# Gated mix of attention and a squared-ReLU layer: phases of six or four scores in place of six or eight, products split over two phases, and VectorE's side work placed by a clock kept while the program is written

## The chip, the cores and the metric

One NeuronCore of a Trainium2 chip runs the whole kernel. The metric is the device time of one execution in microseconds; the times below are those of separate runs of the same program. TensorE (PE), VectorE (DVE), ScalarE (ACT), GpSimd (POOL) and the queue of SyncE (SP) each work through their own list of instructions in the order in which the program wrote them, and wait for one another by semaphores.

## The reference

For 2048 tokens of width 512, one input x goes through two branches, mixed by a gate for each token:

```
g = sigmoid((x * gate_w).sum(-1))
q = x @ wq          # 32 heads of 16
k, v = x @ wk, x @ wv        # one head of 16, shared by all
a = softmax(q k^T * 16**-0.5) v, heads joined, @ wo
h = relu(x @ w1 + b1) ** 2   # 1792 wide
b = h @ w2 + b2
out = g * a + (1 - g) * b
```

All of it is float32; the kernel reaches that accuracy in products by splitting each operand into a rounded part (`r`) and a rest (`l`) and adding three products of them.

## The kernel before, in words

**Attention.** The work is cut into 32 groups (`it`): four heads with 512 tokens of queries each. A group has 32 units `u`: one block of 128 keys against one half (256 columns) of the queries, for all four heads. A unit's score is two matmuls on the two row halves of the array (`r` = 0, 1; `score`, L720), whose results go to a pair of PSUM banks `s` (two buffers; L727) and from there through exp on ScalarE to `e` in SBUF (L751). Some units go another way: each half goes to the single PSUM bank `x`, VectorE copies it to `e` (L738), and exp then runs in place. `context` (L754) multiplies the exps of a block of units with the values and adds in the bank `acc`; it runs four units behind the scores (`AHEAD`).

**Products.** Everything else that TensorE does comes in units of up to twelve products (`pairs`, three for each 128 rows of a term): 15 units for the queries, 56 units `hidden` (L614), `summed` (L635) with twelve or nine products, and the output projection (`outproj`, L199). Each unit's products run on row half 0 in one phase, and again, with the other 64 rows, on half 1 in the next, while the following unit takes half 0. So in each place of a phase two matmuls run side by side: a *pair* of scores, or of products.

**Phases.** `phase` (L1028) writes one phase: at its head a side step or two, then the pairs of scores and products by a text from `PLANS` for (scores, products), in which `S0` is a score, `M` a product, `02`/`12` the two halves of unit 2 for `x`, and `t` a place for VectorE's side work (`tick`, L595); last the exps in a given order. At the end `done` of the unit that has run on both halves reads its bank `mm` on VectorE. Then the caller writes the context of the block. `block` (L1096) says how many units that is: eight in stretches with room, otherwise six, four near the end of a group, and two at the kernel's end. A phase of eight sends its units 4 and 5 through `x`. Where no plan fits, `plain` puts a score every fourth place.

**Side work.** VectorE also splits weights (`w_rest`, L461; ScalarE rounds them first, L468), splits inputs loaded again (`x_again`, L656) and attention results (`ask`), and divides finished groups by their sums in six parts of four instructions (`divide`, L769-L776, called by `pieces`). `tick` takes one job at each `t`; the divisions go one part for each call of `steps_aside` at a phase's head. A job that follows a load waits until a rough clock, which counts phases, has moved on by 6 us.

**Queues.** SyncE issues the loads of weights (L451), of the queries (`q_load`, L424: eight loads at each group's start), and the moves of a finished group's sums (`unpack`, L195, which waits for ScalarE's copy `accs`). Also the load of `ress` into `ot` for the projection (`ahead`, L205; in the trace `big<-ress`), issued at the head of the phase in which the unit's second half runs; its reader is L208.

Of the kernel before, what the change touches and what calls it, by code (L numbers as in the profile page):

```python
# [35 lines left out]
LANDS = 6.0  # L36
GROUPS = (0, 1, 2, 3), (4, 5, 6, 7), (8, 9, 10), (11, 12, 13)
AHEAD = 4
PLANS = {
# [115 lines left out]
def mix_kernel(ctx: ExitStack, tc: tile.TileContext, xT, wkv, wq, wo, w12, b1, b2, cst, out):  # L155
# [42 lines left out]
    def outproj(c, ots, orr, orl, wor, wol):  # L198
        for j in range(4):  # L199
            cols = slice(j * 128, (j + 1) * 128)  # L200
            s = 4 * c + j
            ot = ots[j % 2]

            def ahead(j=j, ot=ot):
                nc.sync.dma_start(ot, ress[c][:, j])  # L205

            def done(p, s=s, ot=ot):
                nc.vector.scalar_tensor_tensor(ot, p, g[:, s:s + 1], ot, op0=OP.mult, op1=OP.add)  # L208
# [10 lines left out]
    with fast, tc.tile_pool(name="at", bufs=1) as at, \  # L219
# [159 lines left out]
        def q_unit(c, t):  # L379

            def done(p):
# [3 lines left out]
                sq = sq8[:, c % 2 * KT + t]  # L385
                nc.vector.tensor_tensor(sq, qr.bitcast(F32), qr.bitcast(F32), OP.mult)
# [51 lines left out]
        clock = 0.0  # L438

        def w_load(half):  # L440
            n = len(wf[half])
            if n < NC * NF:
# [7 lines left out]
                since[half][n] = clock  # L450
# [4 lines left out]
        def w_round(half, copy):  # L455
# [3 lines left out]
            copy(rounded[half][n][0], wf[half][n])  # L459

        def w_rest(half):  # L461
            n = len(ws[half])
            r, l = ws[half][n] = rounded[half][n]
            nc.vector.tensor_tensor(l, wf[half][n], r.bitcast(F32), OP.subtract)
            wanted.append(half)
# [12 lines left out]
        def w_ready(half):  # L478
            n = len(rounded[half])
            return (n == len(ws[half]) and n in since[half] and n < min(room[half], NC * NF)  # L480
                    and clock - since[half][n] > LANDS)
# [77 lines left out]
        for t in (2, 3):  # L559
# [13 lines left out]
        chores, soon = [], [lambda: wq_rest(3), lambda: k_shift(2), lambda: (k_shift(3), w_load(0), w_load(1)),  # L573
                         lambda: (wq_round(0), wq_rest(0))]
        soon += [lambda: (w_load(0), w_load(1))] + [lambda k=k: x_split(2, k) for k in range(KT)]
        soon += [lambda k=k: x_split(3, k) for k in range(KT)] + [gate]
        ring, h, b2t, x, osp = [], [], [], dict(enumerate(zip(xr, xl))), {}

        def later(f, *args):
            chores.append(lambda: f(*args))  # L580
# [5 lines left out]
        def steps_aside(n):  # L586

            for _ in range(n):
                if side and next(side[0], "end") == "end":
                    side.pop(0)  # L590

        def rests():
            return [half for half in halves() if len(rounded[half]) > len(ws[half])]

        def tick(early):  # L595

            nonlocal held
            if soon:
                if early:
                    soon.pop(0)()  # L600
                    if soon and len(es) > 16:
                        soon.pop(0)()
                return
            if not early:
                for half in rests()[:1]:
                    return w_rest(half)
            if chores and clock > held:
                if chores.pop(0)():
                    held = clock + 6.0
# [4 lines left out]
        def hidden(c, f, hs):  # L614
# [3 lines left out]
            while c not in x:  # L618
                chores.pop(0)()
# [3 lines left out]
            def done(p):  # L623
# [3 lines left out]
                split(hr, hl, h[0])  # L627
                room[0] += 1
# [27 lines left out]
        def x_again(c):  # L656
# [11 lines left out]
            for k in range(KT):  # L668
                if k % 2 == 0:
                    chores.append(lambda k=k: load(k // 2))  # L670
# [34 lines left out]

        parts, copied, fifth = {}, {}, [None] * 4
# [20 lines left out]
        def score_part(u, r):  # L727

            if u not in parts:
                parts[u] = [sp.tile([128, 2, CH], F32, name="s"), 0]  # L730
            score(u, r, parts[u][0][:, r])
            parts[u][1] += 1

        def score_copy(u, r):

            x = aside()
            score(u, r, x)
            nc.vector.tensor_copy(e_half(u)[:, 2 * r:2 * r + 2], x.rearrange("p (a n) -> p a n", a=2))  # L738
            copied[u] = copied.get(u, 0) + 1

        def exps(todo):

            while todo:
                u = todo[0]
                if copied.get(u) == 2:
                    src = e_half(u)
                elif u in parts and parts[u][1] == 2:
                    src = parts[u][0].rearrange("p r (a n) -> p (r a) n", a=2)
                else:
# [4 lines left out]
        def context(acc, us):  # L754

            while us:
                u, (it, kt, q) = us[0], place(us[0])
                n = 2 if u % 2 == 0 and len(us) > 1 and it < NC * NG - 1 else 1
                us = us[n:]
                cols, mine = slice(q * HC, (q + n) * HC), slice(u % 2 * HC, (u % 2 + n) * HC)  # L760
                for h in range(4):
                    nc.tensor.matmul(acc[h * 32:(h + 1) * 32, cols], v_ext[:, kt],  # L762
                                     es[u // 2][:, h % 2 * 2 + h // 2, mine], start=(kt == 0), stop=(kt == NK - 1),
                                     skip_group_check=True, tile_position=(0, h * 32))

# [3 lines left out]
        def divide(t, o, l, cols, okc):  # L769

            n = at.tile([128, 86], F32, name="n")[:, :cols.stop - cols.start]
            nc.vector.tensor_scalar(n, l[:, cols], L_MIN, L_MAX, op0=OP.max, op1=OP.min)
            nc.vector.scalar_tensor_tensor(l[:, cols], n, 1.0, l[:, cols], op0=OP.mult, op1=OP.is_equal,  # L773
                                           accum_out=okc)
            nc.vector.reciprocal(n, n)  # L775
            nc.vector.tensor_tensor(o[:, cols], o[:, cols], n, OP.mult)  # L776

        def finish(it, acc):
# [9 lines left out]
            nc.scalar.activation(a, acc, AF.Copy)  # L788
            if u == 0:
                ol[c, t] = [at.tile([128, CH], F32, name=n) for n in ("oc", "lc")]  # L790
            o, l = ol[c, t]
            unpack(nc.sync, o[u * 64:u * 64 + 64], l[u * 64:u * 64 + 64], a)
            if u == 1:
                side.append(pieces(it, c, t, o, l))

        def pieces(it, c, t, o, l):
            for _ in range(2):
                yield
            for q, cols in enumerate(PARTS):
                i = len(PARTS) * (4 * c + t) + q  # L800
                divide(t, o, l, cols, ok[:, i:i + 1])
                if q < len(PARTS) - 1:
                    yield
            nc.gpsimd.dma_start(oTs[it - 1:it + 1].rearrange("u d n -> (u d) n"), o)
            complete.add((c, t))
# [3 lines left out]
        def turn(a, u, js, okc, idle=0):  # L809
# [8 lines left out]
            for j in range(m):  # L818
                nc.tensor.transpose(tp[:, j], a[:, j * 128:(j + 1) * 128], ident)
                if m > 2 and j % 2:  # L820
                    yield
# [55 lines left out]
        def o_ready(c):  # L877

            if c == 0 and not wos:
# [6 lines left out]
                for t in range(KT):  # L886
                    if t % 2 == 0:
                        chores.append(lambda t=t: load(t // 2))
                    chores.append(lambda t=t: split(wos[0][:, t], wos[1][:, t], stage()[:, t % 2]))
# [3 lines left out]
        def ask(c, n=KT):  # L893
# [21 lines left out]
            for t in range(n):  # L915
                if t % 2 == 0:
                    chores.append(lambda t=t: load(t // 2))
                later(part, t)

        def ask_one(c, t):  # L920
# [14 lines left out]
            chores.extend((load, part))  # L935
# [83 lines left out]
        phases, scored, before, evicted = 0, 0, None, None  # L1019
# [8 lines left out]
        def phase(unit, n):  # L1028

            nonlocal phases, scored, before, evicted, clock  # L1030
            halves_of = (unit[0] if unit else ()), (before[0] if before else ())
            slots = max(map(len, halves_of))
            if unit and len(unit[0]) > 6:
                units_left[0] -= 1
            clock += 0.36 + 0.429 * n + 0.2345 * (n + slots)
            full = slots > 8
            tick(True)
            steps_aside(2 if full else 1)
            if narrow:
                qnorm(narrow.pop(0))  # L1040
            if before and before[1][1]:
                before[1][1]()
            if before and not (unit and evicted):
                nc.vector.tensor_copy(at.tile([128, 1], F32, name="peek"), before[2][:, :1])  # L1044
            here = mp.tile([128, CH], F32, name="mm") if unit else None
            text, order = PLANS.get((n, slots)) or plain(n, slots)
            rows, ticks, done = ([], []), {}, [0, 0]
            for item in text.split():
                if item == "t":
                    ticks[len(rows[0])] = True  # L1050
                elif item[0] == "0":
# [8 lines left out]
            def product(r):  # L1060

                i = done[r] - (slots - len(halves_of[1]) if r else 0)
                done[r] += 1
                if 0 <= i < len(halves_of[r]):
                    a, b = halves_of[r][i]
                    p = slice(64 * r, 64 * r + 64)
                    nc.tensor.matmul(before[2] if r else here, a[p], b[p], start=not r and i == 0,  # L1067
                                     stop=r == 1 and i == len(halves_of[r]) - 1, skip_group_check=True)

            for i in range(len(rows[0])):  # L1070
                for r in range(2):
                    item = rows[r][i]
                    if item == "M":
                        product(r)
# [5 lines left out]
                if i in ticks:  # L1080
                    tick(False)
# [3 lines left out]
            phases += 1  # L1085
            evicted = before
            if before:
                before[1][0](before[2])
            before = (unit[0], unit[1:], here) if unit else None
# [6 lines left out]
        def block(u, unit):  # L1096

            k = u % (2 * NK)
            rest = 2 * NK - k
            if u >= total - 2 * NK:  # L1100
                rest = NK - u % NK
# [89 lines left out]
```

## Time and profile before

| | us |
|---|---|
| median of 3 runs | 1315.5 |
| lowest, highest | 1312.73, 1318.16 |
| the profiled execution's own time | 1312.76 |
| its span in the trace | 1311.0 |
| busy: PE, ACT, DVE | 1255.7, 1065.5, 760.4 |

The span runs from the first to the last instruction of the trace; the execution's time is 1.8 us longer. PE's busy time counts every moment in which at least one matmul is recorded as running. In the chain of waits a line gives the start, the length, the engine, the tile that is written and the line of the kernel; in grouped waits a row gives the waiting instruction, what it waited for, the sum in us, the number of times and the longest.

### The profile page before, as it was taken

What the parts mean: (1) busy time and instruction counts of PE and PEld (TensorE: products, weight loads), DVE (VectorE), ACT (ScalarE), POOL (GpSimd) and SP (SyncE); (2) the same over time, 40 slices, a digit from 0 to 9 for tenths busy, and PEclk for the clock granted to TensorE, in tenths of its full rate; (3) what the DMA queues carried; (4) which work ended last, traced back from release to release, by engine and by line L of the source; (5) the groups of instructions that cost most, each with busy time, mean ns of one, the idle gap of its engine ahead of it and who ended that gap; (6) DMA issues with size and microseconds to landing.
All of it is one profiled execution on the core that took longest, in us unless ns stands there. A gap on an engine that the chain in (4) does not pass through costs nothing.

```text
span 1311.0 us, 24220 instructions
## 1 busy us (share of the span) xinstructions
PE 1255.7 (96%) x9839; PEld 673.7 (51%) x9839; DVE 760.4 (58%) x1461; ACT 1065.5 (81%) x1193; POOL 58.7 (4%) x75
## 2 busy tenths in 40 slices
PE   9899899999999999999989998999999999999997
PEld 4555455455545555554545555554555555555454
DVE  5564775657384843738456663655738376464632
ACT  5676788888878888788978887888888888878875
POOL 1010110000001000000002000000000100000000
PEclk9999999999999999999999999999999999999999
DMA  6233521211132213102122222111112121211010
GB/s 207 85 99 80 154 70 30 67 48 52 35 109 78 77 53 102 41 22 78 45 86 82 68 77 78 45 53 46 57 63 69 53 86 38 86 47 37 22 50 35
DMA packets 46117, 88.72 MB, mean 68 GB/s; under 512 B 10642, under 2 KB 10898, under 8 KB 45488
## 3 DMA queue, kind: packets, MB, share of 16 engines
q1 hardware_dynamic: 38752, 71.42, 17.6%
q0 software_dynamic: 7104, 15.44, 3.4%
q8 instruction: 79, 1.29, 0.4%
q14 instruction: 38, 0.31, 0.1%
q10 hardware_dynamic: 144, 0.26, 0.1%
HBM read 57.83 MB, written 20.97 MB: 60 GB/s over the span
## 4 chain that ended last, share of the span: by engine, by line
PE 68%; DVE 12%; ACT 12%; issue 3%; DMA 3%; SPq 1%; ACTq 0%; DVEq 0%
PE acc L762 24%; PE mm L1067 23%; PE s L724 14%; ACT e L751 10%; PE x L724 5%; DVE n L775 2%; DVE e L738 2%; SPq L424 1%; DVE lc L773 1%; DVE big L625 1%; DVE big L626 1%; DMA lc<-accs 1%; DMA big<-ress 1%; ACT w2r L468 1%; DVE hr L184 1%
## 5 line engine op out<-in xcount | busy, mean ns | idle before, releaser
L751 ACT ACTIVATE e<-s 128x1024 f32<-128x1024 f32 x826 | 804.4, 1027 | 217.7 <-PE s L724 126.6
L738 DVE COPY e<-x 128x512 f32<-128x512 f32 x396 | 273.5, 691 | 392.4 <-PE x L724 302.8
L762 PE MATMUL acc<-e,v_ext 128*32 128x512 f32 (+1 forms) x4224 | 475.1, 585 | 0.0
L724 PE MATMUL s<-qa,k_aug 49*128 49x512 f32 x1652 | 431.6, 437 | 14.2 <-ACT e L751 13.4
L724 PEld LDWEIGHTS s<-qa,k_aug 49*128 49x128 f32 x1652 | 208.6, 186 | 224.2 <-ACT e L751 187.8
L762 PEld LDWEIGHTS acc<-e,v_ext 128*32 128x32 f32 x4224 | 121.1, 110 | 259.0 <-issue 255.3
L1067 PE MATMUL mm<-w2r,hr 64*128 64x512 f32 x896 | 219.6, 395 | 0.1
L751 ACT ACTIVATE e<-e 128x1024 f32<-128x1024 f32 x198 | 209.9, 1060 | 0.0
L724 PE MATMUL x<-qa,k_aug 49*128 49x512 f32 x396 | 164.5, 415 | 22.2 <-DVE e L738 19.3
L1067 PEld LDWEIGHTS mm<-w2r,hr 64*128 64x128 f32 x896 | 130.5, 187 | 14.6 <-DVE peek L1044 0.6
L1067 PE MATMUL mm<-w2l,hr 64*128 64x512 f32 x448 | 135.4, 395 | 0.0
L724 PEld LDWEIGHTS x<-qa,k_aug 49*128 49x128 f32 x396 | 74.4, 188 | 54.0 <-DVE e L738 41.3
L1067 PE MATMUL mm<-xragain,w1r 64*128 64x512 f32 x224 | 70.5, 399 | 5.5 <-DVE big L208 5.5
L1067 PEld LDWEIGHTS mm<-w2l,hr 64*128 64x128 f32 x448 | 71.9, 186 | 6.3
L1067 PE MATMUL mm<-xragain,w1l 64*128 64x512 f32 x224 | 74.3, 399 | 0.0
L1067 PE MATMUL mm<-xr,w1l 64*128 64x512 f32 x224 | 72.8, 398 | 0.0
L1067 PE MATMUL mm<-xlagain,w1r 64*128 64x512 f32 x224 | 70.5, 397 | 0.0
L1067 PE MATMUL mm<-xr,w1r 64*128 64x512 f32 x224 | 67.8, 396 | 1.9 <-DVE big L208 1.9
L1067 PE MATMUL mm<-xl,w1r 64*128 64x512 f32 x224 | 68.4, 395 | 0.0
L775 DVE RECIPROCAL n<-n 128x86 f32<-128x86 f32 x90 | 61.9, 688 | 3.1
L648 DVE SCALAR_TENSOR_TENSOR res<-mm,omg,res 128x512 f32<-128x512 f32 x64 | 47.8, 746 | 14.1 <-PE mm L1067 13.9
L625 DVE TENSOR_SCALAR big<-mm,b1t 128x512 f32<-128x512 f32 x56 | 41.8, 746 | 9.8 <-PE mm L1067 9.8
(156 smaller groups left out, 1123.1 us busy)
## 6 DMA issues: line engine op xcount, KB each, us to landing
stage<-in_w SPq DMA_DIRECT2D x56, 256.0 KB
qa<-qs SPq DMA_DIRECT2D x186, 64.0 KB
w1f<-in_w SPq DMA_DIRECT2D x28, 256.0 KB
w2f<-in_w SPq DMA_DIRECT2D x28, 256.0 KB
qs<-qr SPq DMA_DIRECT2D x16, 256.0 KB
ress<-res POOLq DMA_DIRECT2D x4, 1024.0 KB, 4.3
qs<-ql POOLq DMA_DIRECT2D x15, 256.0 KB, 8.2
oc<-accs SPq DMA_DIRECT2D x30, 128.0 KB
```

What stands on the lines that cost most here:

```text
L184: nc.vector.tensor_tensor(l, src, r.bitcast(F32), OP.subtract)
L424: nc.sync.dma_start(q[64 * r + row:64 * r + row + b - a].bitcast(F32), qs[it, r, a:b])
L468: nc.scalar.activation(out, src, AF.Copy)
L625: nc.vector.tensor_scalar(h[0], p, b1t[:, f:f + 1], 0.0, op0=OP.add, op1=OP.max)
L626: nc.vector.tensor_tensor(h[0], h[0], h[0], OP.mult)
L648: nc.vector.scalar_tensor_tensor(part, p, omg[:, s:s + 1], part, op0=OP.mult, op1=OP.add)
L724: nc.tensor.matmul(dst.rearrange("p (a n) -> p a n", a=2), k_aug[rows, kt * 128:(kt + 1) * 128], qa[it][rows, :, q * HC:q * HC + HC], star ...
L738: nc.vector.tensor_copy(e_half(u)[:, 2 * r:2 * r + 2], x.rearrange("p (a n) -> p a n", a=2))
L751: nc.scalar.activation(e_half(u), src, AF.Exp, scale=SCALE)
L762: nc.tensor.matmul(acc[h * 32:(h + 1) * 32, cols], v_ext[:, kt], es[u // 2][:, h % 2 * 2 + h // 2, mine], start=(kt == 0), stop=(kt == NK ...
L775: nc.vector.reciprocal(n, n)
L1067: nc.tensor.matmul(before[2] if r else here, a[p], b[p], start=not r and i == 0, stop=r == 1 and i == len(halves_of[r]) - 1, skip_group_ch ...
```

## The change

Phases have six scores or four; none has eight. A unit's products are no longer bound to one phase: a `Span` holds the unit on half 0 and the one before it on half 1, and `phase(slots, n, m)` takes all its product places (`WHOLE`, with six scores) or half of them (`FIRST` and `SECOND`, with four scores each). `block` decides by how many units of attention and of products are left: a counter `halved` grows with the surplus, and at 1 a span is halved. Every plan sends one unit of four or six through `x`, and its exp comes last or second to last. The first phase writes six scores and takes the next one four.

While the program is written, three numbers (`at_pe`, `at_act`, `at_dve`) count the time of each engine by fixed prices. The `t` places are gone; before each copy of `x`, before a unit's bank is read, and after a phase without such a copy, `spend(until)` writes side work whose end fits before that moment. A division is four jobs in place of one part. Rounding of weights can go to VectorE when ScalarE has no room. `ahead` is issued from GpSimd, at the start of the span in which its unit takes half 0. The phases of the whole program: before, 47 phases of eight scores with twelve products, 8 of eight with nine, 71 of six with twelve, 17 of six with nine; now 80 of six with twelve, 23 of six with nine, 85 of four with six, and some smaller ones.

```diff
 PLANS = {
-    (8, 12): ("S0 M 04 S1 M M M M M S2 M t 14 S3 M M M M 05 M t M S6 M S7 15", (0, 1, 2, 3, 4, 6, 7, 5)),
-    (6, 12): ("S0 M M S1 02 M t M M M M S3 M t 12 M M S4 M M S5", (0, 1, 3, 4, 2, 5)),
+    (6, 12, WHOLE): ("M 02 S0 M S1 M M M M M S3 M M M S4 12 M M S5", (0, 1, 3, 4, 5, 2)),
+    (4, 6, FIRST): ("M 02 S0 M M S1 M M M 12 S3", (0, 1, 3, 2)),
...
             def ahead(j=j, ot=ot):
-                nc.sync.dma_start(ot, ress[c][:, j])
+                nc.gpsimd.dma_start(ot, ress[c][:, j])
...
+        def spend(until=None):
+            nonlocal held
+            def fits(d, ready=0.0):
+                return until is None or max(at_dve, ready) + d <= until
+            while True:
+                due = [i for i in halves() if len(rounded[i]) > len(ws[i])]
+                if due and fits(0.68, since[due[0]][len(ws[due[0]])]):
+                    w_rest(due[0])
+                elif soon and fits(soon[0][1]):
...
+                elif divisions and fits(*divisions[0][:2]):
+                    d, ready, f = divisions.pop(0)
+                    dve(d, ready)
+                    f()
+                elif chores and fits(chores[0][0], held):
+                    d, f = chores.pop(0)
+                    dve(d, held if d else 0.0)
+                    if f():
+                        held = max(at_dve, at_pe) + 6.0
+                else:
+                    return
...
         def score_copy(u, r):
+            nonlocal at_pe
+            at_pe = max(at_pe, used_x[0] + 0.05)
             x = aside()
             score(u, r, x)
+            spend(at_pe + PAIR + 0.27 + LATE)
+            made[u] = used_x[0] = dve(COPY, at_pe + PAIR + 0.27) + 0.06
             nc.vector.tensor_copy(e_half(u)[:, 2 * r:2 * r + 2], x.rearrange("p (a n) -> p a n", a=2))
...
             if u == 0:
+                while divisions:
+                    divisions.pop(0)[2]()
                 ol[c, t] = [at.tile([128, CH], F32, name=n) for n in ("oc", "lc")]
...
             for half in halves():
-                if not soon and w_ready(half):
-                    w_round(half, scalar_copy)
+                if spans > 5 and w_ready(half):
+                    if at_act + 0.64 < at_pe + 0.7 + CONTEXT * m:
+                        w_round(half, scalar_copy)
+                    elif at_dve + 1.2 < at_pe + 0.7 + CONTEXT * m:
+                        w_round(half, nc.vector.tensor_copy)
...
+            if span.done[0] == 0 and left > 9:
+                halved[0] += max(0.0, (total - 56 - u - 6 * units_left[0]) / (1.6 * max(units_left[0], 1)))
+            if rest == 8 or rest == 4 or left > 9 and halved[0] >= 1.0 and rest != 6:
+                halved[0] -= 1.0
+                return 4, (left + 1) // 2
+            return min(rest, 6), left
```

**What moved on TensorE.** Before, the second part of a phase of eight in the first stretch of `summed` and the start of the next phase (`s` x2 is a score in two banks, `x` half a score, `mm` products, `acc` the context):

```order
L724 MATMUL x<-qa,k_aug 128x512
L724 MATMUL s<-qa,k_aug 128x512 x2
L1067 MATMUL mm<-w2l,hr 128x512 x2
L1067 MATMUL mm<-w2r,hr 128x512 x4
L1067 MATMUL mm<-w2l,hr 128x512 x2
L724 MATMUL x<-qa,k_aug 128x512
L1067 MATMUL mm<-w2r,hr 128x512 x2
L724 MATMUL s<-qa,k_aug 128x512 x4
L724 MATMUL x<-qa,k_aug 128x512
L762 MATMUL acc<-e,v_ext 32x512 x12
L762 MATMUL acc<-e_2059,v_ext 32x512 x4
```

Now, the first half of a span of two `hidden` units, with its context of four units:

```order
L1102 MATMUL mm<-xr_80,w1r 128x512 x2
L761 MATMUL x<-qa,k_aug 128x512
L761 MATMUL s<-qa,k_aug 128x512 x2
L1102 MATMUL mm<-xl_84,w1r 128x512 x2
L1102 MATMUL mm<-xr_80,w1l 128x512 x2
L761 MATMUL s<-qa,k_aug 128x512 x2
L1102 MATMUL mm<-xr_80,w1r 128x512 x2
L1102 MATMUL mm<-xl_84,w1r 128x512 x2
L1102 MATMUL mm<-xr_80,w1l 128x512 x2
L761 MATMUL x<-qa,k_aug 128x512
L761 MATMUL s<-qa,k_aug 128x512 x2
L812 MATMUL acc<-e,v_ext 32x512 x8
```

The last half-score for `x` was the last thing before the context and had another a few places ahead of it; now a phase has two of them, and a score and no `x` stands last.

**What moved on VectorE.** Before, in the third chunk of the MLP, after a `hidden` unit's last split (L184): two parts of a division (L772-L776), a copy of `x`, a weight's rest (L464), a copy of `x`, and the next unit's bank (L625):

```order
L184 TENSOR_TENSOR hr<-big,hr 128x512
L772 TENSOR_SCALAR n<-lc 128x86
L773 SCALAR_TENSOR_TENSOR lc,ok<-n,lc 128x86
L775 RECIPROCAL n<-n 128x86
L776 TENSOR_TENSOR oc<-oc,n 128x86
L772 TENSOR_SCALAR n<-lc 128x86
L773 SCALAR_TENSOR_TENSOR lc,ok<-n,lc 128x86
L775 RECIPROCAL n<-n 128x86
L776 TENSOR_TENSOR oc<-oc,n 128x86
L738 COPY e_10404<-x 128x2x256
L464 TENSOR_TENSOR w1l<-w1f,w1r 128x512
L738 COPY e_10404<-x 128x2x256
```

Now, in the same chunk after such a split (L192):

```order
L192 TENSOR_TENSOR hr<-big,hr 128x512
L490 TENSOR_TENSOR w1l<-w1f,w1r 128x512
L826 TENSOR_SCALAR n<-lc 128x86
L782 COPY e<-x 128x2x256
L829 SCALAR_TENSOR_TENSOR lc,ok<-n,lc 128x86
L832 RECIPROCAL n<-n 128x86
L833 TENSOR_TENSOR oc<-oc,n 128x86
L826 TENSOR_SCALAR n<-lc 128x86
L829 SCALAR_TENSOR_TENSOR lc,ok<-n,lc 128x86
L782 COPY e<-x 128x2x256
```

A division's four instructions stand on both sides of a copy; ahead of the first copy are the weight's rest and one short instruction in place of eight.

**What moved between the queues.** Before, SyncE at a group's end: the moves of the sums, eight loads of queries, then `ress`:

```order
L195 DMA oc<-accs 64x512
L196 DMA lc<-accs 64x512
L424 DMA qa<-qs 16x1024 x3
L424 DMA qa<-qs 1x1024
L424 DMA qa<-qs 16x1024 x3
L424 DMA qa<-qs 1x1024
L205 DMA big<-ress 128x512
```

Now, GpSimd around a projection, with the outputs (L217) and a finished division's result (L859):

```order
L213 DMA big<-ress 128x512 x2
L217 DMA out<-big 128x512
L213 DMA big<-ress 128x512
L217 DMA out<-big 128x512
L213 DMA big<-ress 128x512
L217 DMA out<-big 128x512 x2
L859 DMA oTs<-oc 128x512 x3
```

The loads of `ress` stand between the outputs on GpSimd; two are ahead of the first output.

More of the change, by code (lines that the diff above doesn't have):

```diff
@@ L1039, in phase @@
+        def phase(slots, n, m):
+            nonlocal scored, evicted, at_pe
+            step_aside()
             if narrow:
+                used_x[0] = dve(1.3) + 0.06
                 qnorm(narrow.pop(0))
[L1041 to L1045, printed above, removed]
@@ L1084, in phase @@
             scored += n
[L1085 to L1089, printed above, removed]
+            if not span.left():
+                evicted = span.before
+                if evicted:
+                    spend(at_pe + 0.3)
+                    dve(0.76, at_pe + 0.3)
+                    evicted.unit[1](evicted.bank)
+            if not any(item[0] == "0" for item in text.split()):
+                spend(at_pe)
             while wanted:
@@ L1140, in mix_kernel @@
         while side:
[L1141 to L1146 removed]
+            step_aside()
+        spend()
+        while span.unit:
+            fetch()
+            phase(span.slots, 0, 0)
         for _ in half(acc, 1):
```

246 lines of the change are left out of this document (140 added, 106 removed), and 2 rows, old and new, of the table PLANS.

## The prediction

> **What bounds the kernel now.** I read the profile's page first, then the chain of waits in an undisturbed and in a disturbed stretch, then the grouped waits, and last the timelines of single places. The page:
>
> ```profile
> span 1311.0 us, 24220 instructions
> PE 1255.7 (96%) x9839; PEld 673.7 (51%) x9839; DVE 760.4 (58%) x1461; ACT 1065.5 (81%) x1193; POOL 58.7 (4%) x75
> ```
>
> And the context matmuls, asked for by line (shortest, median and longest duration in ns; first and last start in us):
>
> ```profile
> L762 PE MATMUL acc<-e,v_ext x4224: 379/592/1061, 40.2 to 1299.6; 128*32 128x512 f32 x181, 128*32 128x256 f32 x11
> ```
>
> The phases run from 40.2 to about 1299.9 us, 1259.7 us of the 1311.0. TensorE looks full. But busy is not work here. Two neighbours on one half of the array, 14 pairs apart in the timeline of PE:
>
> ```profile
> 1110.05 0.40 PE L1067 MATMUL mm<-w2r,hr 64*128 64x512 f32 x1
> ...
> 1113.32 0.39 PE L1067 MATMUL mm<-w2l,hr 64*128 64x512 f32 x1
> ```
>
> Each shows 0.40 us, yet 14 pairs start within 3.27 us: a pair costs 0.234 us, and records overlap, so a stalled engine can look busy. The chain of waits has the other prices (start, length; each x24 is the context of six units, x32 of eight):
>
> ```profile
> 1114.20 2.71 PE acc L762 x24
> 1121.32 2.71 PE acc L762 x24
> 1128.45 2.72 PE acc L762 x24
> 1135.59 2.72 PE acc L762 x24
> ```
>
> A context costs (3.57 - 2.71) / 2 = 0.43 us a unit (3.57 from the x32 rows below). A clean phase of six with twelve products lasts 7.13 us; less 18 pairs (4.21) and six contexts (2.58) leaves 0.34 us for the turn. So the bare time of a phase is 0.234 x (scores + products) + 0.43 x units + 0.34.
>
> From the first context on, before writes 1014 scores and 1731 product pairs in 162 further phases, and 1024 units of context: 642.3 + 440.3 + 55.1 = 1137.7 us. Measured 1259.7. **122.0 us are stalls**; this is what can be won. Where are they?
>
> ```profile
> 183.62 0.70 DVE e L738
> 184.37 0.49 PE x L724
> 184.86 3.57 PE acc L762 x32
> ...
> 194.22 3.57 PE acc L762 x32
> ...
> 212.88 3.57 PE acc L762 x32
> ...
> 221.87 3.57 PE acc L762 x32
> ...
> 230.86 1.40 PE acc L762 x9
> ```
>
> Eights in the chain: 9.36 us apart at first, 8.99 at the end, against a bare 20 x 0.234 + 3.44 + 0.34 = 8.46: they lose 0.53 to 0.90, because the last half-score for x waits until VectorE has copied the half before it out of the one x bank (DVE e, then PE x, then the context). There are 55 eights (47 with twelve products, 8 with nine). At 0.85 each, with the disturbed ones: 47 us.
>
> The stretch of the query products, 15 phases (11 sixes, 4 fours):
>
> ```profile
> 42.90:160.00 117.10, 108.36 (x873) 58.72 (x869) 71.61 (x135) 85.45 (x97) 11.29 (x15) 1.00 0.39 112
> ```
>
> Bare 11 x 7.13 + 4 x 5.80 = 101.6, so 15.5 us lost. The remaining 59 us lie in sixes and at the end, and look like this (timeline of VectorE, then of PE):
>
> ```profile
> 1004.21 0.20 DVE L772 TENSOR_SCALAR n<-lc 128x86 f32<-128x86 f32 x1
> ...
> 1007.00 0.25 DVE L776 TENSOR_TENSOR oc<-oc,n 128x86 f32<-128x86 f32 x1
> 1007.17 0.68 DVE L738 COPY e<-x 128x512 f32<-128x512 f32 x1
> ```
>
> ```profile
> 1007.91 0.49 PE L724 MATMUL x<-qa,k_aug 49*128 49x512 f32 x1 [0.42 <-DVE e L738]
> ```
>
> Two divisions (2.96 us) stand ahead of the copy of x on VectorE, and TensorE, which works in order, waits for the bank: the phase takes about 8.0 instead of 7.13.
>
> **The change part by part.** *Turns.* The scores are the same, three product pairs and 43 phases more (205 instead of 162 after the first context): 3 x 0.234 + 43 x 0.34 = **+15.3 us**. Nothing hides a turn on TensorE.
>
> *Eights go.* **-47 us** in stalls; their units come back in halved phases, whose own stalls are priced below.
>
> *VectorE's side work by a clock.* Divisions are cut in four instructions, splits and weights' rests are written where they end at most 0.3 us after the next copy is due. Of the 59 us, three waits belong to another part:
>
> ```profile
> 517.05 0.47 SPq L195 DMA_DIRECT2D oc<-accs  x1
> ...
> 518.21 3.44 SPq L424 DMA_DIRECT2D qa<-qs  x8
> 521.74 0.35 SPq L205 DMA_DIRECT2D big<-ress  x1
> ```
>
> ```profile
> DVE big L208 <- DMA big<-ress: 16.4, 3, 6.5
> PEld mm L1067 <- DVE big L208: 8.3, 3, 3.8
> ```
>
> The load of ress stands behind SyncE's wait for accs and eight loads of q; VectorE waited 16.4 us in three places, TensorE 8.3 and some copies more. The change issues it on GpSimd, and when the unit begins instead of a phase later, so it has some 14 us: **-12 us**, between 8.3 and 16.4, 12 being the middle. It then stands behind GpSimd's waits for the division's last product and for the output that frees ot; with two phases to land, that is cover enough, and if it fails the 12 us stay. The Trainium skill (DMA: Bandwidth & Descriptors, Issuing engines are not separate DMA queues) says that issuing from several engines saves only the issue time, usually small. By it this term would be near 0, and the sum 12 us higher; here the issue is the wait, 4.69 us from the accs copy to the load's issue.
>
> *Roundings.* 42 of the 112 roundings of weights move from ScalarE to VectorE, as casts like this one (grouped view, mean 437 ns):
>
> ```profile
> L183 DVE CAST hr<-big 128x512 fp32r<-128x512 f32 x56 | 24.5, 437 | 1.9
> ```
>
> 18 us more on an engine that is busy 58%: nothing on the path while the copies of x are on time, and part of the late copies below if not.
>
> The other 47 of the 59 us and the 15.5 go in so far as the clock is right. What stays I price by rows:
>
> - Nine-product phases have a floor above bare even when clean:
>
> ```profile
> 332.79 2.71 PE acc L762 x24
> 339.45 2.71 PE acc L762 x24
> ```
>
> 6.66 against 6.43: 23 of them, 5 us.
> - Halved phases, 85 with six products: bare 4.40. Before has only three such fours, unplanned, without x:
>
> ```profile
> 1256.46 1.92 PE L762 MATMUL acc<-e,v_ext 128*32 128x512 f32 x16
> 1261.37 1.92 PE L762 MATMUL acc<-e,v_ext 128*32 128x512 f32 x16
> ```
>
> 4.91 apart, 0.51 over bare. Without x all four scores pass two banks; the new plan gives one of four to x, and its two halves stand seven pairs (1.64 us) apart, room for the copy (0.69) and its hand-overs. So between 0 and 0.51 each, 0 to 43 us; I take 0.1, nearer the clean sixes, which also mix x: 8.5 us. ScalarE fits: four exps at about 0.97 us (two in 1.94, ACT's rows below) in 4.40.
>
> ```profile
> 1005.03 1.94 ACT L751 ACTIVATE e<-s 128x1024 f32<-128x1024 f32 x2 [0.45 <-PE s L724]
> ```
>
> - The query stretch keeps half, 7.5 us (0 to 15.5): it has only four e buffers and the splits of x.
> - One late load as in this row, after which a phase lost more than it: 7 us (0 to 15).
>
> ```profile
> DVE xragain L183 <- DMA stage<-in_xT: 5.0, 1, 5.0
> ```
>
> - Late copies in the 79 sixes: 0 to 0.37 each (29 us, half of the old rate), I take 4. Six times unfinished divisions (4 to 11 instructions) are written in one burst that the clock does not count; that is in the 4.
>
> Together 32 us stay. **Sum, from the profiled execution's own 1312.8 us: 1312.8 - 122.0 + 15.3 + 32 = 1238 us.** The runs' median is 2.7 us above that execution; I take half: 1240.
>
> **The rivals.** *A: the fours cost what the old fours cost.* Then 85 x 0.41 = 35 us more: 1275. For it: the only rows of fours. Against: their bank traffic was another. 0.15.
>
> *B: TensorE is as full as its busy time says.* Then only the idle 55.3 us can go, less 15.3: 1273. For it the page's 96%; against it the overlapping records. The Trainium skill (Perfetto Trace Analysis, Identifying the Most-Contended Engine) holds that busy share of matmuls does not measure the distance from the limit, since they are pipelined; the 0.40 us records 0.234 us apart agree. 0.06.
>
> *C: slower.* Every phase now sends a score through the one x bank, in fours as well, so each of some 200 phases has two copies for which VectorE must come in time. If the real VectorE runs later than the clock (one uncounted burst, one landed-late weight, and all later positions are wrong), each phase loses the 0.87 us of the late phase above (8.0 - 7.13). Break-even: 1312.8 - 122.0 + 15.3 = 1206.1, so 107 us of stalls, or 123 late phases of 202. All of them late: 1206 + 176 = 1382; at 75% late 1338. Against it: VectorE is busy 58%, so it can catch up within a phase or two. 0.07.
>
> *D: no change*: the clock only exchanges which phases are late, and turns eat the eights. 1313. 0.05.
>
> **How the numbers follow.** Forecast 0.67, A 0.15, B 0.06, C 0.07, D 0.05. Faster by over 0.5% (about what this kernel's measurement can tell, since three runs spread over 0.4%): forecast, A and B, 0.88; same 0.05; slower 0.07. Range: the low end takes 12 us of stalls for 32 (nines and little else), 1220; the high end takes in A and B and some late loads, 1284. Outside lie C, D and a tail of each, about 0.2.
>
> **What would show it.** Right: halved phases whose contexts start 4.4 to 4.5 us apart; sixes at 7.1 to 7.2 throughout, also at 43 to 160 us; no DVE wait for ress; PE's wait for DVE at x of a few us. Wrong: fours at 4.8 or more (A), eight-wide waits replaced by DVE e before PE x in the chain of most phases (C), or PE waiting for something else between contexts that none of these rows shows.

## The result and the profile after

| | before | after |
|---|---|---|
| median, us | 1316.8 (4 runs, 1312.7 to 1320.8) | 1244.0 (4 runs, 1241.2 to 1248.4) |
| ratio, 95% interval | | 0.945 (0.941 to 0.949) |
| span of the profiled execution, us | 1311.0 | 1242.0 |

The change makes the kernel 5.5% faster. The page of after, and its context matmuls asked for by line:

```profile
span 1242.0 us, 24097 instructions
PE 1219.7 (98%) x9838; PEld 674.0 (54%) x9839; DVE 767.0 (62%) x1507; ACT 1038.9 (84%) x1151; POOL 67.3 (5%) x87
```

```profile
L812 PE MATMUL acc<-e,v_ext x4224: 379/592/1061, 36.1 to 1229.5; 128*32 128x512 f32 x181, 128*32 128x256 f32 x11
```

The phases now run from 36.1 to about 1229.9 us, 1193.8 us. Their bare time by the prediction's prices is 1153.0, so 40.8 us of stalls are left of 122.0. PE's busy time fell by 36 us although it runs the same matmuls: it had counted stalled and slow matmuls as work.

The chain of waits in a stretch of halved spans and sixes (start, length, each x16 is the context of four units):

```profile
822.86 1.85 PE acc L812 x16
827.24 1.86 PE acc L812 x16
833.55 2.71 PE acc L812 x24
838.83 1.85 PE acc L812 x16
843.23 1.85 PE acc L812 x16
```

From one context's end to the next, a four takes 4.39 us (827.24 + 1.86 less 822.86 + 1.85), against a bare 4.40, and the six after it 7.16. Nothing but TensorE stands in the chain there. The median of all fours with six products is 4.41, of all sixes with twelve 7.14.

Who waited for VectorE's copy of x, before and then after (waiting instruction, what it waited for, us, times, longest):

```profile
PEld x L724 <- DVE e L738: 41.3, 60, 5.2
PE x L724 <- DVE e L738: 19.3, 20, 4.8
```

```profile
PEld x L761 <- DVE e L782: 10.4, 12, 2.6
...
DVE orr L191 <- DMA stage<-oTs: 9.5, 3, 4.9
...
PE x L761 <- DVE e L782: 6.1, 4, 2.2
```

From 80 waits to 16, and VectorE waits for the load of `ress` (`big<-ress`) no more. What remains is in few places. One is a load that VectorE met before it had landed (chain):

```profile
448.54 5.85 DMA qa<-qs
...
454.45 3.54 DMA stage<-oTs
...
458.01 0.44 DVE orr L191
...
459.82 0.61 PE x L761
```

By the chain SyncE's loads of queries had to land before the load of `stage` was issued; that phase took 11.33 us for 7.13. Another is the burst of unfinished divisions at a group's end:

```profile
593.46 0.69 DVE e L782
594.15 0.61 DVE n L832
...
597.83 0.24 DVE oc L833
598.07 0.61 DVE e L782
598.73 0.50 PE x L761
```

Between two copies of x stand 3.9 us of division, and the four took 7.2 us for 3.9.

Part of both losses comes from the clock that TensorE is granted by the chip, which is not the clock that the program keeps. Here is the burst in this execution and in another of the same kernel, the reference below: a row for the stretch, in which the third number from the end is the granted clock, and the context that follows (chain). First this execution:

```profile
600.00:603.40 3.40, 3.40 (x18) 0.93 (x12) 0.61 (x1) 1.71 (x2) 0.00 (x0) 0.50 0.31 111
```

```profile
599.70 3.27 PE acc L812 x16
```

Then the reference:

```profile
598.80:604.60 5.80, 4.39 (x34) 1.97 (x34) 4.08 (x10) 4.49 (x6) 0.54 (x1) 1.00 0.12 46
```

```profile
602.72 1.85 PE acc L812 x16
```

At half clock the context takes 3.27 us for 1.85, and the four 7.23 us for 5.81: of the 3.3 us lost in the burst, 1.4 come from the half clock. Within the phases, before has five such stretches of 3.4 or 6.8 us (20.5 us in all), after has four (17.1 us). Each of the nine follows, or begins in, a gap of 1.3 to 4.8 us in TensorE's work; but the gaps of 1.4 us at the burst and 1.3 us near the end, which one followed here, had none in the reference. So a stall can cost more than the wait, and not the same in every execution.

### The profile page after: what moved, and what is told of

It reads as the page before. It is cut to its first block, busy times and chain, and to the rows that moved or that the text cites. A ratio compares the mean times of both kernels' runs of the same rounds, so it can differ in the third digit from the quotient of the medians.

```text
span 1242.0 us, 24097 instructions
## 1 busy us (share of the span) xinstructions
PE 1219.7 (98%) x9838; PEld 674.0 (54%) x9839; DVE 767.0 (62%) x1507; ACT 1038.9 (84%) x1151; POOL 67.3 (5%) x87
## 4 chain that ended last, share of the span: by engine, by line
PE 90%; ACT 5%; DVE 2%; DMA 1%; issue 1%; SPq 0%; ACTq 0%; DVEq 0%
PE acc L812 35%; PE mm L1102 31%; PE s L761 16%; PE x L761 5%; ACT e L798 4%; DMA stage<-oTs 1%; PE mm L295 0%; DMA qa<-qs 0%; DVE e L782 0%; PE acc L524 0%; PE mm L199 0%; DVE n L832 0%; ACT w1r L495 0%; DVE tmp L347 0%; SPq L433 0%
## 5 line engine op out<-in xcount | busy, mean ns | idle before, releaser
L798 ACT ACTIVATE e<-s 128x1024 f32<-128x1024 f32 x825 | 786.1, 1025 | 176.8 <-PE s L761 158.7
L812 PE MATMUL acc<-e,v_ext 128*32 128x512 f32 (+1 forms) x4224 | 487.4, 590 | 0.0
L761 PE MATMUL s<-qa,k_aug 49*128 49x512 f32 x1650 | 466.4, 414 | 1.8 <-ACT e L798 1.2
L761 PEld LDWEIGHTS s<-qa,k_aug 49*128 49x128 f32 x1650 | 235.8, 185 | 79.5 <-ACT e L798 54.5
L1102 PE MATMUL mm<-w2r,hr 64*128 64x512 f32 x896 | 228.5, 402 | 0.0
L1102 PE MATMUL mm<-w2l,hr 64*128 64x512 f32 x448 | 144.9, 393 | 0.0
L1102 PEld LDWEIGHTS mm<-w2l,hr 64*128 64x128 f32 x448 | 80.8, 186 | 6.8
L1102 PE MATMUL mm<-xragain,w1r 64*128 64x512 f32 x224 | 76.8, 418 | 0.2
L832 DVE RECIPROCAL n<-n 128x86 f32<-128x86 f32 x90 | 61.5, 684 | 2.0
L1102 PEld LDWEIGHTS mm<-xragain,w1r 64*128 64x128 f32 x224 | 38.4, 185 | 28.5 <-issue 11.7
L1102 PEld LDWEIGHTS mm<-xr,w1r 64*128 64x128 f32 x224 | 37.5, 185 | 27.5 <-issue 10.4
```

The source lines that it names most:

```text
L761: nc.tensor.matmul(dst.rearrange("p (a n) -> p a n", a=2), k_aug[rows, kt * 128:(kt + 1) * 128], qa[it][rows, :, q * HC:q * HC + HC], star ...
L798: nc.scalar.activation(e_half(u), src, AF.Exp, scale=SCALE)
L832: return ((0.23, bound), (0.35, compare), (0.72, lambda: nc.vector.reciprocal(n[0], n[0])), (0.28, lambda: nc.vector.tensor_tensor(o[:, co ...
L1102: nc.tensor.matmul((self.before if r else self).bank, a[p], b[p], start=not r and i == 0, stop=r == 1 and i == len(self.terms[1]) - 1, ski ...
```

## The experiments

Every experiment starts from the changed kernel, unless it says otherwise. Losses by kind of phase are sums of the time from one context's end to the next, less the bare time. Stalls, as above, are the time from the first context's start to the last one's end, less the bare 1153.0. The reference, the load back on SyncE, the run without the clock and the eights were measured on one chip, the others on two more, on which before took 1315.4 and 1317.8 us for 1313.4; differences of a few us to the reference are uncertain for that reason.

**The reference.** 

> The changed kernel unaltered, as the reference beside the three others on this chip: 1244 us within 0.3%, span about 1242.

Measured 1242.3 us (1242.0 to 1244.3), ratio to before 0.944 (0.939 to 0.949), span 1240.4, stalls 38.8 us. The runs below are compared with this.

The granted clock accounts for nearly all of the spread between runs. The seven runs of before beside this one took 1310.4 to 1321.7 us; each multiplied by its mean granted clock (0.981 to 0.990) they lie between 1296.0 and 1298.2. The eight runs of the changed kernel, here and above, took 1241.2 to 1248.4 us, and so multiplied 1232.1 to 1234.7. By this estimate, which counts half of each half-clock stretch as lost even where TensorE waited in it, some 64 of the 73 us gained would be there at full clock as well; the rest comes with fewer stretches at half clock.

**The load of ress back on SyncE.**

```diff
-                nc.gpsimd.dma_start(ot, ress[c][:, j])
+                nc.sync.dma_start(ot, ress[c][:, j])
...
-            if span.unit and span.unit[2]:
-                span.unit[2]()
+            if span.before and span.before.unit[2]:
+                span.before.unit[2]()
```

> The changed kernel with the load of ress back on SyncE and back at the head of the second span. Theory of the prediction (the wait was issue time behind accs and the loads of q): the three kinds of wait return where a projection begins at a group's end; 8 to 16 us slower than the reference if all three places meet a group's end again, 0 to 4 if the new schedule happens to miss them; DVE waits for big<-ress reappear in the waits. Rival (a queue makes no difference to a DMA): no change, no such wait.

Measured 1251.9 us, ratio 0.950 (0.945 to 0.955): 9.5 us slower. SyncE and VectorE around a group's end, and the grouped wait:

```profile
747.36 0.47 SPq L203 DMA_DIRECT2D oc<-accs  x1
...
748.57 3.38 SPq L433 DMA_DIRECT2D qa<-qs  x8
752.04 0.82 SPq L213 DMA_DIRECT2D big<-ress  x2
```

```profile
755.41 0.75 DVE L216 SCALAR_TENSOR_TENSOR big<-mm,g,big 128x512 f32<-128x512 f32 x1 [7.81 <-DMA big<-ress]
```

```profile
DVE big L216 <- DMA big<-ress: 13.1, 3, 7.8
```

The wait is back, behind the accs and the eight loads. One phase there lost 8.5 us; TensorE's granted clock was 0.50 for 6.8 us of it, so up to 3.4 us of the loss come from the half clock.

**The same part alone, on the kernel before.**

```diff
-                nc.sync.dma_start(ot, ress[c][:, j])
+                nc.gpsimd.dma_start(ot, ress[c][:, j])
...
-            if before and before[1][1]:
-                before[1][1]()
+            if unit and unit[2]:
+                unit[2]()
```

> The kernel before with one part of the change alone: the load of ress issued from GpSimd and at the head of the phase in which its unit starts on half 0. Theory of the prediction: the 16.4 us of VectorE's waits for big<-ress go and with them 8 to 13 us of time, 1302 to 1308 against 1315. Rival (a queue makes no difference to a DMA): no change.

Measured 1305.2 us beside 1317.8 for before, ratio 0.9913 (0.988 to 0.995): about 11.5 us faster, 7 to 16. The waits for `big<-ress` are gone from its list. The two runs together show the term and its size of 12. In both the queue and the moment of issue were moved together; which of the two does it, and whether an earlier issue on SyncE would have been enough, is not tested.

**No clock.**

```diff
             def fits(d, ready=0.0):
-                return until is None or max(at_dve, ready) + d <= until
+                return until is None or ready <= at_pe
-            while True:
+            jobs = 0
+            while until is None or jobs < 1:
+                jobs += 1
...
                 elif divisions and fits(*divisions[0][:2]):
-                    d, ready, f = divisions.pop(0)
-                    dve(d, ready)
-                    f()
+                    for _ in range(min(4, len(divisions))):
+                        d, ready, f = divisions.pop(0)
+                        dve(d, ready)
+                        f()
```

> The changed kernel with the clock taken out of the placing: at each of the same places VectorE gets exactly one job, a whole part of a division counted as one, whether it fits or not. Phases and plans are unchanged. Theory of the prediction: late copies of x return at the old rate, 0.4 us on each of the 79 sixes with twelve products and something like it on the fours: 25 to 60 us slower than the reference, with DVE e before PE x in the chain of waits. Rival (the gain comes from the phases alone, the clock is decoration): at most 5 us slower.

Measured 1265.7 us, ratio 0.961 (0.956 to 0.966): 23.4 us slower, just under the range and far above the rival. Stalls are 62.0 for 38.8: +13.5 in the sixes, +6.2 in the fours, +4.3 in the query stretch, and a little less elsewhere. VectorE, then PE, where it shows best:

```profile
180.96 1.05 DVE L192 TENSOR_TENSOR wol<-stage,wor 128x512 fp32r<-128x512 f32 x1
181.94 0.68 DVE L785 COPY e<-x 128x512 f32<-128x512 f32 x1
```

```profile
182.67 0.50 PE L764 MATMUL x<-qa,k_aug 49*128 49x512 f32 x1 [0.79 <-DVE e L785]
```

PE's waits for the copy of x rise from 18 to 36 in all, not to the 80 of before.

**Eights put back.**

```diff
 PLANS = {
+    (8, 12, 0): ("S0 M 04 S1 M M M M M S2 M 14 S3 M M M M 05 M S6 S7 15", (0, 1, 2, 3, 4, 6, 7, 5)),
...
                 halved[0] -= 1.0
+                if q_over and span.done[0] == 0 and rest >= 8 and rest not in (10, 12):
+                    return 8, left
                 return 4, (left + 1) // 2
```

> The changed kernel with 24 phases of eight scores and twelve products put back, by the old plan's order of scores and products, each in place of two halved phases; the clock stays. Theory of the prediction (an eight loses at least 0.53 us to the single x bank whatever VectorE does): an eight takes 8.99 or more against 2 x 4.40, so 4 to 13 us slower than the reference. Rival (eights lost time only because VectorE's jobs stood in the way): they fall to the bare 8.46 and save a turn each, 24 x 0.34 = 8 us faster.

Measured 1250.6 us, ratio 0.951 (0.946 to 0.956): 8.3 us slower. The chain:

```profile
559.72 1.72 PE acc L814 x16
566.92 3.57 PE acc L814 x32
```

From end to end this eight takes 9.05 us; the median of the 24 is 9.04. Two fours take 8.82, so the 24 cost 24 x 0.22 = 5.3 of the 8.3 us; the rest lies in other phases. VectorE's copy of the third half for x, and the wait for it of the last half, in this eight:

```profile
565.68 0.69 DVE L784 COPY e<-x 128x512 f32<-128x512 f32 x1 [0.73 <-PE x L763]
...
566.04 0.18 PEld L763 LDWEIGHTS s<-qa,k_aug 49*128 49x128 f32 x2 [0.37 <-ACT e L800]
566.43 0.18 PEld L763 LDWEIGHTS x<-qa,k_aug 49*128 49x128 f32 x1 [0.20 <-DVE e L784]
```

The copy starts 0.04 us after the half-score ahead of it (565.25 to 565.64) and the last half starts 0.06 us after the copy. So with VectorE on time an eight keeps 0.58 us over its bare 8.46, more than the turn it saves; a wait for an exp, which frees an s buffer, stands just ahead and ends earlier.

**Fours without x.**

```diff
-    (4, 6, FIRST): ("M 02 S0 M M S1 M M M 12 S3", (0, 1, 3, 2)),
+    (4, 6, FIRST): ("S0 M M S1 M M S2 M S3 M", (0, 1, 2, 3)),
```

(and so for the other plans of four)

> The changed kernel with all four scores of the fours in the two s buffers, spread over the products, none through x; sixes unchanged. Theory of the prediction (the old fours cost 4.91 because four scores pass two buffers): fours go from 4.41 towards 4.6 to 4.9, 17 to 40 us slower than the changed kernel's 1242. Rival (the fours are bound by TensorE alone, the way through x is not needed there): within 3 us.

Measured 1300.1 us, ratio 0.988 (0.985 to 0.991): 58 us slower, more than the theory's own range. The chain of this run:

```profile
701.28 1.90 PE acc L812 x16
...
703.69 1.94 ACT e L798 x2
...
706.41 1.85 PE acc L812 x16
```

A four now takes 5.08 us here (median 5.12) instead of 4.41, and an exp on ScalarE stands in the chain between two contexts: a score waits for an s buffer, and that for an exp. The grouped wait, in the reference and then in this run:

```profile
PEld s L761 <- ACT e L798: 54.0, 146, 0.9
```

```profile
PEld s L761 <- ACT e L798: 199.5, 351, 1.6
```

The way through x is what makes the short phase possible.

**The old order in the sixes.**

```diff
-    (6, 12, WHOLE): ("M 02 S0 M S1 M M M M M S3 M M M S4 12 M M S5", (0, 1, 3, 4, 5, 2)),
-    (6, 9, WHOLE): ("S0 M 03 M S1 M M M S2 M M M S4 13 M S5", (0, 1, 2, 4, 5, 3)),
+    (6, 12, WHOLE): ("S0 M M S1 02 M M M M M S3 M 12 M M S4 M M S5", (0, 1, 3, 4, 2, 5)),
+    (6, 9, WHOLE): ("S0 M 03 S1 M M M S2 M M M 13 M S4 M S5", (0, 1, 2, 4, 5, 3)),
```

> The changed kernel with the old order of scores and products in the sixes (first half for x at the fifth place instead of the second, second half seven places later, unit 2's exp before unit 5's); clock, fours and all else stay. Theory of the prediction (the clock alone keeps the copies on time): within 5 us of the changed kernel's 1242. Rival (the new order, which puts the two halves for x fourteen places apart, takes part of the gain): 10 to 25 us slower, and the sixes of the query stretch near their old 7.85.

Measured 1249.6 us, ratio 0.950 (0.946 to 0.953): 7.3 us slower, between the two. The loss lies in the query stretch, 14.8 for 8.1 us, and there nearly all in one phase at 42.3 us (6.9). There TensorE stood idle for 4.0 us and then ran at half clock, as it had at the start:

```profile
32.10:38.90 6.80, 6.80 (x33) 5.47 (x34) 1.35 (x4) 3.30 (x4) 0.00 (x0) 0.50 0.12 30
45.70:52.50 6.80, 6.15 (x28) 3.51 (x32) 5.57 (x10) 3.52 (x4) 0.90 (x1) 0.50 0.38 120
```

The next run has the old order too, and loses 0.4 in that phase. In the 72 later sixes stalls are 1.5 us, fewer than with the new order (8.4, of which 6.7 is one late load). So the order does not matter where most sixes are, and that it does at the start is not shown. The four runs (1245.7 to 1251.9) overlap with the changed kernel's (1241.2 to 1248.4); multiplied by their granted clock they are some 3 us slower, which is within the theory's 5.

**Both taken back: no clock, old order.** 

> The changed kernel with both taken back: one job at each place without the clock, and the old order in the sixes. If the new order made the sixes bear late copies (the two halves for x fourteen places apart), the loss is more than the sum of the two alone (23 and 6 us): 1280 or more, the sixes at a mean of 7.6. If clock and order are independent: 1268 to 1275.

Measured 1269.5 us, ratio 0.963 (0.960 to 0.967); stalls 61.5 for the 62.0 without the clock alone. The loss is no more than the sum of the two; the idea that the new order protects the sixes from late copies falls.

**Roundings on ScalarE.**

```diff
                     if at_act + 0.64 < at_pe + 0.7 + CONTEXT * m:
                         w_round(half, scalar_copy)
-                    elif at_dve + 1.2 < at_pe + 0.7 + CONTEXT * m:
-                        w_round(half, nc.vector.tensor_copy)
```

> The changed kernel without the choice that sends roundings of weights to VectorE; those for which ScalarE has no room wait for a later phase, and are done on VectorE only when a unit needs them. Theory of the prediction (18 us of casts on an engine with room cost nothing): within 3 us of the changed kernel's 1242. Rival (ScalarE's exps pay for the roundings): 5 to 15 us slower.

Measured 1260.9 us, ratio 0.958 (0.954 to 0.961): 18.5 us slower. My theory falls; the rival's number is near, but its mechanism is not what the trace shows. VectorE at the start of a `summed` unit:

```profile
258.84 0.69 DVE L490 TENSOR_TENSOR w2l<-stage,w2r 128x512 fp32r<-128x512 f32 x1
261.12 0.43 DVE L481 CAST w2r<-w2f 128x512 fp32r<-128x512 f32 x1 [1.58 <-DMA w2f<-in_w]
...
263.53 0.68 DVE L782 COPY e<-x 128x512 f32<-128x512 f32 x1
```

Weights that were not rounded in time are made all at once when the unit begins (27 roundings still end on VectorE), and each pair waits for its load, which could not start before the previous weight was done; the copy of x stands behind them, and that phase lost 3.5 us. Stalls rise from 38.8 to 55.6; ScalarE is busy 1048 us of 1257. The run shows what it costs when a weight must wait for room on ScalarE by the clock and has no other way. It does not show what before's rule would cost here, by which ScalarE rounds all 112 whether it has room or not; that stays untested.

**Divisions let through earlier.**

```diff
+            def urgent():
+                g, k = divmod(scored - AHEAD, 2 * NK)
+                return 0.6 if g % 2 == 0 and k > 6 else 0.0
...
-                elif divisions and fits(*divisions[0][:2]):
+                elif divisions and fits(divisions[0][0] - urgent(), divisions[0][1]):
```

> The changed kernel with divisions let through up to 0.6 us later than the clock allows in the groups at whose end they would be written in a burst; the bursts shrink from 41 instructions in six places to 3 in one. Theory (the burst of 11 costs 3.3 us, the smaller ones less): 3 to 6 us faster than the changed kernel's 1242. Rival (each division placed late costs what the burst did): 0 to 3 us slower.

Measured 1236.5 us, ratio 0.940 (0.937 to 0.942): 5.8 us faster than the reference. The number is as expected; the reason given holds only in part. The phase of the burst loses 0.25 us for 1.9 in the reference. More comes from the load at 454 us, which landed earlier, so that VectorE waited less for it; first the reference, then this run:

```profile
459.56 0.43 DVE L191 CAST orr<-stage 128x512 fp32r<-128x512 f32 x1 [6.03 <-DMA stage<-oTs]
```

```profile
456.73 0.43 DVE L191 CAST orr<-stage 128x512 fp32r<-128x512 f32 x1 [2.73 <-DMA stage<-oTs]
```

That phase loses 0.4 us for 6.7; in the reference TensorE ran at half clock for 6.8 us of it. Whether the earlier divisions do this is not shown: in the two executions of the changed kernel the wait is 4.9 and 6.0 us.

**And a longer hold after a load.**

```diff
-                        held = max(at_dve, at_pe) + 6.0
+                        held = max(at_dve, at_pe) + 9.0
```

> The same with the hold after a load raised from 6 to 9 us of the clock, so that VectorE does not meet stage<-oTs before it has landed. Theory (the two waits at 454 and 1121 us cost TensorE 4 and 3.6 us): another 5 to 8 us faster, 1230 to 1236 in all. Rival (later jobs only move the collision, the projection then starts later): no faster than without the longer hold.

Measured 1233.2 us, ratio 0.937 (0.934 to 0.939): 3.3 us more, below the 5 to 8 expected but in the total's range: of the two waits that it was to remove, the first cost little any more in the run above. The second, which cost that run 3.9 us, is gone. No wait for `stage` is left in its list, and its page reads:

```profile
span 1232.9 us, 24096 instructions
PE 1215.5 (99%) x9839; PEld 675.9 (55%) x9839; DVE 763.9 (62%) x1506; ACT 1039.9 (84%) x1152; POOL 64.8 (5%) x87
```

Stalls are 30.9 us; the largest parts are some 8 in the query stretch, 6 in the nine-product phases and 10 at the end, where TensorE ran at half clock for 6.8 us. This version beats both kernels.

## Why the prediction was right, point by point

The forecast was 1240, the median 1244.0. The profiled execution took 1243.7 against 1238 in the sum. The difference is made of 8.8 us more stalls (40.8 for 32), 4.1 us less ahead of the first context (36.1 for 40.2) and 1.1 us more after the last (12.1 for 11.0), so that the forecast came this close is in part luck.

- **Turns, +15.3.** Bare time after is 1153.0, measured clean phases are within 0.03 of it. Right.
- **Eights, -47.** Right in kind: put back, 24 of them cost 5.3 us, because each keeps 0.58 us over bare even with the clock. The 0.85 taken for the old ones also held late copies.
- **Load of ress, -12.** Right in size: -11.5 alone on before, +9.5 when undone. That 12 is the middle of 8.3 and 16.4 had no reason of its own; the three phases with these waits lost 3.7, 5.3 and 3.8 us in before, and in each TensorE ran at half clock for 3.4 us. The Trainium skill's rule (DMA: Bandwidth & Descriptors, Issuing engines are not separate DMA queues), by which the sum would be 12 us higher, did not hold here: what was saved is time ahead of the issue, as the rule says, but it was 4.69 us at one group's end and not small.
- **The clock.** Of the 122.0 the eights and the load of ress take 59, which leaves 63 to this step; 32 were to stay. The run without the clock has 62.0, the reference 38.8: the clock is worth 23 us of the 31 expected. The other parts of the side work need it and each other, and do not simply add: some 18 us are lost when weights must wait for ScalarE to round them, and I had priced the roundings at nothing. Single waits that were longer before (as for the load of `xragain`, 5.0 us for VectorE, 2.1 after) may be part of the rest; that is not separated.
- **What stays, 32.** Measured 40.8. Nines 5.8 for 5; query stretch 8.1 for 7.5; the late loads 4.2 and 3.6, together 7.8 for 7; the burst 3.3 of the 4 for late copies; the clean fours nothing for 8.5. What has no term is the end: from 1194 us on the phases lost 9.6, where before's last ones lost some 5. The four stretches at half clock lie in the late loads, the burst and the end. They have no term either; up to 8.5 us of the 40.8, half of their 17.1, are theirs.
- **Not priced: the head.** The first context starts at 36.1 for 40.2. Most of this is the granted clock, before's row first, then after's:

```profile
31.00:38.00 7.00, 5.65 (x27) 4.11 (x28) 3.04 (x8) 2.05 (x2) 0.00 (x0) 0.51 0.14 39
```

```profile
31.00:38.00 7.00, 6.79 (x55) 3.77 (x58) 6.20 (x14) 4.15 (x5) 0.07 (x1) 1.00 0.42 136
```

The run with the load back on SyncE shares after's head and had 0.50 from 31.3 to 38.1 us; its first context ends at 41.5, after's at 38.9, before's at 42.9. So of the 4.0 us some 1.4 are the change and 2.6 the granted clock, which in the experiments with this head was now half, now full.

Of the signs named beforehand, fours 4.4 apart and no wait for ress came. Sixes at 7.1 to 7.2 also from 43 to 160 us did not: there they took 7.14 to 8.58. And TensorE's waits for the copy of x are 16.5 us in all, down from 60.6, more than a few.

Of the rivals, A (fours at 4.9) was wrong here because of x, as its counter-argument said, and the run without x shows that it was the real danger: with 5.12 the whole gain but 1.2% is gone. B fell: after is shorter by 69 us although only 55.3 were idle. C did not happen; the copies waited for fell from 80 to 16. D fell.

## What to carry to other kernels

Price a phase by the starts of its instructions, add up what the bare phases would take, and compare with the span: the difference is what can be won, whatever the busy share says. A short phase is only as good as the way its results leave: keep the detour that frees the buffer and check it by taking it out. And look at what an in-order queue has ahead of a load before calling the load slow; when placing side work by a clock, count every instruction that is written, the bursts too. When two runs of one kernel differ, look at the granted clock of each stretch before looking for a cause in the code.

## What the runs showed of the hardware that was not expected

While GpSimd ran its products for `res` (1.75 us each, three in a row from 177.1 us), VectorE's instructions in the run without the clock grew longer:

```profile
177.08 5.26 POOL L684 TENSOR_SCALAR res<-big,omg 128x512 f32<-128x512 f32 x3 [10.05 <-DMA big<-in_b]
```

```profile
179.33 0.98 DVE L192 TENSOR_TENSOR hr<-big,hr 128x512 fp32r<-128x512 f32 x1
180.23 0.69 DVE L191 CAST wor<-stage 128x512 fp32r<-128x512 f32 x1
```

While GpSimd does nothing, VectorE's two-input instructions of this form take 0.70 us at most in this run, its casts 0.43. The Trainium skill (SBUF — State Buffer, SBUF: two separate sides) holds that VectorE and GpSimd share a pair of ports, which one of them holds for a whole instruction while the other is blocked. The trace agrees that they hinder one another, but not for a whole instruction: VectorE started seven instructions in these 5.26 us, and those that grew lost about 0.3 us, not GpSimd's whole 1.75.
